# Normalizing half of the Hedgehog features by a ratio of two sums, with other landing margins in the kernel's planner

## The chip, the cores and the metric

The kernel runs on one core of a Trainium2 chip. The metric is the device time of one execution in microseconds (us). Before the change it is 823.11 us, the median of 5 runs that lie between 822.02 and 823.58 us. The profiled execution is one of these runs and took 823.16 us. Its span in the profile, from the first to the last instruction, is 821.4 us, so 1.76 us lie around it.

Names of engines: PE is the matrix engine (PEld its weight loads), ACT the activation engine, DVE the vector engine, POOL the GpSimd engine, SP the engine that issues most transfers.

## The reference: what is computed

One sequence of S = 2048 tokens, width D = 512, H = 32 heads of 16 elements. Two attention branches read the same input `x`, and a gate mixes them: `out = g * a + (1 - g) * b` with `g = sigmoid(sum(x * gate_w))` per token.

- Branch A is ordinary attention: `p = softmax(q k^T / 4)`, `o = p v`, then the output projection. Its 32 x 2048 x 2048 exponentials are most of the work.
- Branch B is linear attention with Hedgehog features. For each head, `pq = q @ w_phi` and `pk = k @ w_phi` have 16 elements. The features are two softmaxes of 16 elements, laid side by side: `phi = [softmax(p), softmax(-p)]`. Then

```python
kv  = einsum("bhsf,bhsd->bhfd", phi_k, v)      # 32 x 16 for each head
z   = phi_k summed over the tokens
num = einsum("bhqf,bhfd->bhqd", phi_q, kv)
den = einsum("bhqf,bhf->bhq", phi_q, z)[..., None] + 1e-6
o   = num / den
```

So each head's feature row has two sums to divide by: s+ of the 16 `exp(p)` and s- of the 16 `exp(-p)`.

## The kernel before, in words

**Branch A, the main chain** (`main_chain`). The work is cut into 32 pieces (a group of four heads and a quarter of the queries), each piece into 16 key tiles of 128 keys, each key tile into four units of 128 keys x 512 queries, one for a head. For two units at a time PE writes scores into two of the four banks of `ps_ring` (line 932), ACT turns them into exponentials in `ET` (line 950, one instruction for 128x1024), and PE multiplies `ET` by the values into `ps_ot` (line 989). The score pair k waits for exponential k-2, because it overwrites its banks. ACT and PE thus run in lockstep with a lead of about one exponential.

**The second way to an exponential** (`dve_pack`). `DVE_COUNT` says for each of the 32 pieces how many of its 16 key tiles don't go to ACT. For such a tile PE writes the scores into a bank of `ps_mp` (line 1039), DVE scales them into a 32-bit integer `EW` (line 1044), POOL or DVE makes the fraction `Ef` of it (line 1073), POOL the exponent part `ED` (line 1077), DVE evaluates a polynomial (lines 1082, 1084, 1086), and an accumulating DMA that POOL issues adds `Ef` to `ED` (line 1089). PE then multiplies `ED` by the values (line 1100). Each such tile takes four units, two exponentials, from ACT.

**Branch B** (`branch_b`, `feature`, `query_b`) runs beside this. For each of 16 token tiles, for keys first and then for queries, `feature` projects (line 773) and ACT writes `exp(p)` and `exp(-p)` into `phi` (line 1241, two instructions). The sums are made by PE: a transposing DMA on SP puts `phi` into `phiT` (line 1260), eight small matmuls with `ind8` give 64 sums for each token (line 1250), DVE takes 64 reciprocals (line 1253) and multiplies all 1024 elements of `phi` (line 1254). For keys, V is projected and copied to `VB` (line 1194) beside a column of ones, eight groups of 65 columns, and PE accumulates `phi^T VB` (line 1204) over four token tiles. For queries `phi` is transposed a second time, PE multiplies it by `kvz` (denominators) and `kvbd` (numerators), and lines 1285, 1288 and 1289 divide. The result is transposed by another DMA into `onT_B` (line 1294).

The three banks of `ps_mp` are shared by all of this: projections, sums, scores for `dve_pack`, and output blocks.

**The order of the work** is not written by hand. When the program is built, a list scheduler (`Sched.run`) plays through all instructions with a table of durations and fixes the order on each engine. Its settings are the lists at the top of the file: due times and leads (`LEAD`, `PACE`, `OFF`, `PRI`, `POLY`), choices for each piece (`PAIR`: scores for `dve_pack` two at a time; `JOINT`: `ET` products of two key tiles together; `SHAPE`, `FILL`, `SHY`, `AFF`, `SLIP`: how the pieces of `dve_pack` are cut and shared between DVE and POOL). PE may take other work ahead of a score pair when `outlook` (line 164) finds that the pair will still be ready in time. For transfers the planner supposes a landing time after the issue; whatever needs the data is placed on PE's queue by it. The actual program waits on semaphores, so a wrong supposition gives no wrong result, but PE takes its queue in order: when a matmul waits for a late transfer, the score pairs behind it wait too. In the planner before, these landing times are

```python
if o.kind == "acc":
    o.end = max([o.start + (5.5 if turns and o.start - turns[-1] < 1.3 else 4.7)] +
                [a.end + 2.65 for a in accs[-1:]])
...
    o.end = o.start + (4.15 if o.kind == "qT" else 3.05 if o.kind == "phi" else 2.43)
```

Here `acc` is the accumulating DMA, `qT` a set of four transfers that place queries (line 808), `phi` and the last one the two transposes of branch B, and `turns` the starts of the transposes. While a product sum in `ps_ot` is open, PE also fills free time with matmuls of zeros (line 1008, `spare_mm`), as long as fewer than `QUOTA` columns were streamed in the last 3.413 us.

Of the kernel before, what the change touches and what calls it, by code (L numbers as in the profile page):

```python
# [8 lines left out]
ALU = mybir.AluOpType  # L9
AX = mybir.AxisListType  # L10

P = 128
D = 512
H = 32
DH = 16
# [16 lines left out]
LEAD = [30.0, 5.0, 15.587634343078882, 18.596008015614277, 21.09664890476773, 40.540151693083416, 4.700229106743385, 13.0]  # L32
PACE = [0.9342151336517385, 0.45790104673263465]
BOUNDS = [3.0710501327799653, 8.000889564597248, 7.98930768224379, 18.02257936663145, 29.86797202712817]
RULES = [0.1498235423970469, 0.5274031413498357, 0.11548542575895482]
# [3 lines left out]
AFF = [4.15497164884861, 0.18343314021531576, 3.4899946808590343, 2.3674940671931393, 0.0, 2.90437474412157, 0.7415344049336196, 3.2417994652524023, 0.0, 0.04936235801504704, 0.5936669881661917, 3.1602669851720693, 0.0, 0.0, 0.44709012098761747, 0.0, 2.1406325166983535, 2.5346731449762023, 0.21204954920410735, 0.0, 3.3400645974699685, 0.22787943080925754, 0.5055877317539534, 0.0, 0.7354200939583246, 2.786126368892715, 1.0743845299433354, 0.7132921107694127, 3.722000841705053, 0.0, 0.0, 0.0, 0.0]  # L39
PAIR = [1, 0, 0, 0, 0, 0, 0, 0, 0, 0, 0, 0, 0, 0, 0, 0, 0, 0, 0, 1, 1, 1, 0, 0, 1, 1, 1, 0, 1, 1, 1, 0, 0]  # L40
JOINT = [0, 0, 1, 1, 0, 1, 0, 1, 1, 0, 1, 0, 1, 0, 0, 1, 1, 0, 1, 0, 0, 0, 0, 1, 0, 0, 1, 0, 0, 0, 1, 0, 0]
SWD = [0.65, 662500, 1.85]
CLEAR = [3.0, 1.2, 0.97]
OFF = [0.0, -0.8897703043510494, 0.5172481291637241, -1.6001482920023302, 2.691800625687394, -4.61876105583856, 9.931835604720934, 3.749480399812751, -2.5354011754586376, 6.457003779301287, 5.486868139035972, -6.13598057955875, 6.241188808437798, -4.516210493380233, -4.720084637924602, 5.808771137792029, -0.362969914738815, 5.451969429638361, -0.20710302246636036, 1.602535412833622, -2.7420692773393607, 6.8960641134545035, -1.5364304379614095, -4.520043988488846, -1.9086060678527623, 4.191789611328016, 0.0, -10.92683283831524, 7.908073056639142, -2.846662271061698, 1.1690496888958446, 2.378092297094616, 0.0]
PRI = [-2.5977761809841518, 12.575398704445774, 3.895376356683779, 11.515588944229506, -9.189983291385724, 11.325175017241945, 6.76640473260813, 12.368950578623885, 19.409552720225648, 1.7122892583984095, -5.057883055897609, 4.784017942556362, 8.536057932420114, 0.1302334100251321, 11.794699785256503, 5.62627294606187, -17.665801839387232, -7.161052481135956, -12.903739516547825, 14.835504297642174, 2.941617488397717, -8.594367097189757, 10.157188453890655, -20.005512559792166, -9.773812266304459, 1.8583573414742158, -5.94449476159381, -2.8717857218875027, -2.836104354426574, -2.8974936905181274, -12.357333215935258, 8.557379841186394, 0.0]
# [4 lines left out]
SHAPE = [0, 2, 0, 2, 2, 1, 0, 0, 2, 2, 1, 0, 0, 0, 0, 0, 0, 0, 0, 1, 0, 1, 2, 0, 0, 0, 2, 1, 1, 1, 1, 1, 1]  # L50
VSL = 17

EC = 0.25 * 1.4426950408889634 * 65536
EM = -68
EU = 0.96498297
E1, E3 = 61.15205816, 9.99312212


DVE_COUNT = (1, 3, 4, 2, 3, 3, 3, 3, 1, 3, 3, 4, 2, 3, 3, 3, 3, 4, 4, 3, 3, 3, 3, 3, 4, 3, 3, 3, 3, 3, 3, 4)


def dve_tiles(n):
    return ((6,), (5, 11), (4, 8, 12), (3, 6, 9, 12), (2, 5, 8, 11, 13))[DVE_COUNT[min(n, NN - 1)] - 1]

# [49 lines left out]
class Sched:  # L124
# [6 lines left out]
    TURN = 0.102  # L131
# [32 lines left out]
    def outlook(self, t, now):  # L164
# [6 lines left out]
        r, back = now, None  # L171
# [1238 lines left out]
```

The softmax here doesn't subtract the row's maximum and nothing guards it: scores larger than these inputs give would overflow.

## Time and profile before

| | |
|---|---|
| median of 5 runs | 823.11 us |
| the profiled execution | 823.16 us |
| its span | 821.4 us |
| granted clock of PE | 1.000 |
| ACT busy | 801.2 us, 98% of the span |
| DVE busy | 775.1 us, 94% |
| PE busy | 770.5 us, 94% (matmuls overlap; fillers included) |
| POOL busy | 412.4 us, 50% |
| `ED<-Ef` issue to landing, median | 4.5 us |
| `phiT<-phi` issue to landing, median | 3.1 us |

A row of a group reads: line, engine, operation, destination and source tile, shape, count, then busy time in us and mean ns of one, then the time for which the engine stood idle just before these instructions and what ended most of it. An instruction's own duration includes its overlap with its neighbours on the engine: an exponential lasts 1157 ns, but they follow each other at 773.9 / 832 = 0.93 us. A row of a timeline gives the start, the length of the merged run, the engine, the line, the count, and in brackets the idle time before it with what ended it. A row of waits gives who waited for what, the total in us, how often, and the longest.

### The profile page before, as it was taken

To read this page: it belongs to the slowest core of one execution; us is meant where nothing else is said; L and a number is where in the kernel's file an instruction comes from. 1 tells how busy PE (TensorE), PEld (TensorE's weight loads), DVE (VectorE), ACT (ScalarE), POOL (GpSimd) and SP (SyncE) were. 2 spreads that over 40 slices of the span, in tenths; PEclk is the share of its full clock that TensorE was granted. 3 is DMA by queue.
4 is the path that set the end of the run, shared out by engine and by line. 5 is a ranking of instruction groups with operands and counts; after the bars stand their busy time and mean duration, and the time that the engine had idled before them with its cause. 6 is when DMAs were issued, how large, how long until landed. Compare 5 with 4: busy or idle time off the path is not lost.

```text
span 821.4 us, 15309 instructions
## 1 busy us (share of the span) xinstructions
PE 770.5 (94%) x6131; PEld 236.2 (29%) x6131; DVE 775.1 (94%) x1093; ACT 801.2 (98%) x904; POOL 412.4 (50%) x493
## 2 busy tenths in 40 slices
PE   8999999999999999988999999999899999899998
PEld 3323333233333232222222222222222222222222
DVE  7999989999999999999999998999999999999994
ACT  6999999999999999999999999999999999999997
POOL 3457446455446544554555454465345456555562
PEclk9999999999999999999999999999999999999999
DMA  6572633445545444455445433455544336534343
GB/s 125 118 123 55 129 61 70 87 90 101 100 107 101 87 93 88 90 107 88 93 101 102 101 74 78 82 92 115 102 91 81 74 73 123 95 75 97 71 97 84
DMA packets 96742, 76.38 MB, mean 93 GB/s; under 512 B 76832, under 2 KB 84384, under 8 KB 96672
## 3 DMA queue, kind: packets, MB, share of 16 engines
q0 software_dynamic: 13824, 50.34, 31.1%
q1 hardware_dynamic: 81504, 24.55, 15.1%
q8 instruction: 48, 0.79, 0.4%
q10 hardware_dynamic: 1344, 0.52, 0.3%
q14 instruction: 22, 0.18, 0.1%
HBM read 3.69 MB, written 2.10 MB: 7 GB/s over the span
## 4 chain that ended last, share of the span: by engine, by line
ACT 70%; PE 11%; DVE 10%; DMA 6%; SPq 1%; issue 1%; POOL 0%; ACTq 0%
ACT ET L950 67%; PE ps_ring L932 4%; DVE EW L1044 3%; DMA ED<-Ef 3%; ACT phi L1241 3%; DMA phiT<-phi 2%; PE ps_ot L989 2%; DVE Ef L1086 1%; DVE Em L1082 1%; DMA qT<-qst 1%; PE ps_mp L773 1%; PE ps_mp L1319 1%; PE ps_mp L1039 1%; SPq L808 1%; DVE phi L1254 1%
## 5 line engine op out<-in xcount | busy, mean ns | idle before, releaser
L950 ACT ACTIVATE ET<-ps_ring 128x1024 bf16<-128x1024 f32 x832 | 773.9, 1157 | 8.6 <-PE ps_ring L932 8.4
L932 PE MATMUL ps_ring<-qT,kT 64*128 64x512 bf16 x1664 | 326.3, 386 | 30.5 <-ACT ET L950 19.7
L1077 POOL TENSOR_SCALAR ED<-EW 128x512 int16<-128x512 int16 (+1 forms) x284 | 232.9, 846 | 172.0 <-DVE Em L1082 62.1
L1044 DVE TENSOR_SCALAR EW<-ps_mp 128x512 int32<-128x512 f32 (+1 forms) x326 | 241.3, 775 | 18.0 <-PE ps_mp L1039 15.2
L932 PEld LDWEIGHTS ps_ring<-qT,kT 64*128 64x128 bf16 x1664 | 80.2, 93 | 296.7 <-ACT ET L950 274.7
L1073 POOL TENSOR_SCALAR Ef<-EW 128x1024 f16<-128x1024 uint16 (+1 forms) x105 | 94.9, 904 | 106.3 <-DVE Ef L1086 36.9
L989 PE MATMUL ps_ot<-ET,Vaug 128*17 128x512 bf16 x1664 | 146.9, 383 | 0.2 <-DVE T L1129 0.2
L1089 POOL DMA_DIRECT2D ED<-Ef x96 | 87.5, 912 | 117.8 <-DVE Ef L1086 65.6
L1082 DVE TENSOR_TENSOR Em<-Ef 128x2048 f16<-128x2048 f16 x96 | 121.5, 1266 | 0.6 <-POOL Ef L1073 0.2
L1008 PE MATMUL ps_ot<-zero,iden 64*128 64x512 bf16 (+2 forms) x570 | 120.7, 377 | 0.0
L1086 DVE TENSOR_TENSOR Ef<-Ef,Em 128x2048 int16<-128x2048 f16 x96 | 120.2, 1252 | 0.3
L1039 PE MATMUL ps_mp<-qT,kT 64*128 64x512 bf16 (+1 forms) x384 | 112.3, 381 | 7.2 <-DMA qT<-qst 2.5
L1073 DVE TENSOR_SCALAR Ef<-EW 128x1024 f16<-128x1024 uint16 (+1 forms) x123 | 75.8, 628 | 0.1
L1084 DVE TENSOR_SCALAR Em<-Em 128x2048 f16<-128x2048 f16 x96 | 71.5, 745 | 0.1
L989 PEld LDWEIGHTS ps_ot<-ET,Vaug 128*17 128x17 bf16 x1664 | 33.4, 87 | 75.9 <-issue 69.7
L1039 PEld LDWEIGHTS ps_mp<-qT,kT 64*128 64x128 bf16 (+1 forms) x384 | 30.0, 94 | 48.0 <-DVE EW L1044 18.6
L773 PE MATMUL ps_mp<-Wp,xT 128*128 128x512 bf16 x128 | 41.2, 384 | 0.1
L1100 PE MATMUL ps_ot<-ED,Vaug 128*17 128x512 bf16 x384 | 37.7, 383 | 3.6 <-DMA ED<-Ef 3.4
L1008 PEld LDWEIGHTS ps_ot<-zero,iden 64*128 64x128 bf16 (+2 forms) x570 | 35.9, 94 | 17.5
L773 PE MATMUL ps_mp<-xT,WA 128*128 128x512 bf16 (+1 forms) x128 | 38.9, 380 | 0.3 <-ACT xT L757 0.3
L1254 DVE TENSOR_TENSOR phi<-phi,ps_mp 128x1024 bf16<-128x1024 bf16 x32 | 38.6, 1208 | 0.4
L1241 ACT ACTIVATE phi<-ps_mp 128x512 bf16<-128x512 f32 x64 | 38.6, 722 | 0.0
(90 smaller groups left out, 401.0 us busy)
## 6 DMA issues: line engine op xcount, KB each, us to landing
ED<-Ef POOLq DMA_DIRECT2D x96, 512.0 KB, 4.5
qT<-qst SPq DMA_DIRECT2D x120, 16.0 KB, 1.8
out_dram<-outt SPq DMA_DIRECT2D x12, 128.0 KB, 1.7
WA<-in_A_wqkv_dram SPq DMA_DIRECT2D x3, 384.0 KB, 4.4
phiT<-phi SPq DMA_TRANSPOSE x48, 3.1
WBV<-in_B_wqkv_dram SPq DMA_DIRECT2D x1, 512.0 KB, 4.3
Wp<-in_A_wo_dram SPq DMA_DIRECT2D x1, 512.0 KB, 3.9
WBV<-in_B_wo_dram SPq DMA_DIRECT2D x1, 512.0 KB, 4.8
```

The costliest lines, as they stand in the source:

```text
L773: m = s.op("pe", self.c_mm(n), lambda e, c=c: e.matmul(self.bk(b)[:, 0:n], lhs(c), rhs(c), start=(c == 0), stop=(c == 3)), deps if c == 0 ...
L932: return lambda e: e.matmul(self.ps_ring[:, x % RING, :], self.kT[r, g // 2, kt * P:(kt + 1) * P], self.qT[r, n % 2, i, :], start=True, st ...
L950: self.o_exp.append(s.op("act", w * 0.434 + 0.039, lambda e, b0=b0, s0=s0, w=w: e.activation(self.ET[:, s0:s0 + w, :], self.ps_ring[:, b0: ...
L989: return lambda e: e.matmul(self.ps_ot[32 * i:32 * i + VSL, :], self.Vaug[:, kt, h, :], self.ET[:, (4 * p + k) % NSLOT, :], start=(kt == 0 ...
L1008: return lambda e: e.matmul(self.ps_ot[c:c + nc, :], self.iden[r:r + nr, 0:nc], self.zero[r:r + nr, :], start=False, stop=False, tile_posi ...
L1039: return lambda e: e.matmul(bank(), self.kT[r, cp, kt * P:(kt + 1) * P], self.qT[r, n % 2, i, :], start=True, stop=True, tile_position=(r. ...
L1044: return s.op("dve", dur, lambda e: e.tensor_scalar(self.EW[:, ew.idx, x * QCH:(x + w) * QCH].rearrange("p (b q) -> p b q", b=w) if w > 1 else
L1073: fs = [s.op("pool", U * 8.26e-4 + 0.28, lambda e, c=c: e.tensor_scalar(self.Ef[:, ef.idx, U * c:U * c + U], half(0, dt.uint16, c, U), flo ...
L1077: hs = [s.op("pool", W * 8.26e-4 + 0.165, lambda e, c=c: e.tensor_scalar(self.ED[:, ed.idx, W * c:W * c + W].bitcast(dt.int16), half(1, dt ...
L1082: u = s.op("dve", 1.13, lambda e: e.tensor_tensor(self.Em[:], Ef(), Ef(), ALU.mult), fs + [self.ed_prev], pr, port=True)
L1086: g_ = s.op("dve", 1.13, lambda e: e.tensor_tensor(Ef().bitcast(dt.int16), Ef(), self.Em[:], ALU.mult), [q], pr, port=True)
L1089: v = s.op("pool", SWD[0], lambda e: e.dma_start(out().bitcast(dt.int16), Ef().bitcast(dt.int16), accum_op=ALU.add), [g_] + hs, pr, frees= ...
```

## The change

In branch B, let s+ and s- be the two sums of a feature row, and r = s- / s+.

- `feature` no longer multiplies all 1024 elements of `phi` by reciprocals. It multiplies only the `exp(p)` half (512 elements) by r, so that both halves lack the same factor 1 / s-. A new small instruction makes r, in free columns of the same bank of `ps_mp`.
- For keys the missing 1 / s- is put on V: the copy to `VB` becomes a multiplication by it, and the column of ones becomes four columns that hold 1 / s- for the four heads of a group (65 columns become 68). So the copy now needs the reciprocals, which stay in a new buffer `rcp` with two slots.
- For queries the factor cancels in num / den, apart from the 1e-6, which is multiplied by s- (new instruction into `sm`) and added together with the gate's factor.
- In the planner the supposed landing times become `CLEAR[3:7]`: 4.85 us for an accumulating DMA, 0.7 us more when a transpose started less than 2.4 us (before: 1.3 us) earlier, 3.26 us for `phi`, 5.2 us for `qT`, 2.6 us for `onT`. `outlook` keeps a further 0.05 us (`CLEAR[7]`) ahead of a score pair, a score pair is costed at 0.2225 instead of 0.2155 us, and `QUOTA` falls from 6000 to 5200 columns.
- `DVE_COUNT` is another list: nine of the 32 pieces change, and the sum goes from 96 to 95 key tiles.
- The settings `AFF`, `PAIR`, `JOINT`, `OFF`, `PRI`, `SHY`, `FILL`, `SLIP`, `POLY` and `SHAPE` get other values for many pieces, and three entries of `LEAD`, `PACE` and `RULES` small changes; these rows are left out below.

```diff
-CLEAR = [3.0, 1.2, 0.97]
+CLEAR = [3.0, 1.2, 0.97, 4.85, 3.2623642462425315, 5.2, 2.6, 0.05]
...
-DVE_COUNT = (1, 3, 4, 2, 3, 3, 3, 3, 1, 3, 3, 4, 2, 3, 3, 3, 3, 4, 4, 3, 3, 3, 3, 3, 4, 3, 3, 3, 3, 3, 3, 4)
+DVE_COUNT = (1, 3, 4, 3, 3, 3, 2, 2, 1, 3, 3, 4, 2, 4, 3, 3, 3, 4, 4, 2, 4, 2, 3, 4, 3, 3, 3, 3, 3, 3, 3, 4)
...
-        return q, r, a - self.TAIL["pe"] - q.dur
+        return q, r, a - self.TAIL["pe"] - q.dur - CLEAR[7]
...
-                    o.end = max([o.start + (5.5 if turns and o.start - turns[-1] < 1.3 else 4.7)] +
+                    o.end = max([o.start + (CLEAR[3] + 0.7 if turns and o.start - turns[-1] < 2.4 else CLEAR[3])] +
                                 [a.end + 2.65 for a in accs[-1:]])
...
-                    o.end = o.start + (4.15 if o.kind == "qT" else 3.05 if o.kind == "phi" else 2.43)
+                    o.end = o.start + CLEAR[{"phi": 4, "qT": 5, "onT": 6}[o.kind]]
...
-    TICK, QUOTA = 3.413, 6000
+    TICK, QUOTA = 3.413, 5200
...
-            o_qk = s.op("pe", 0.2155 if w < 3 else 0.431, [qk(x, w > 1) for x in range(ua, ub + 1)],
+            o_qk = s.op("pe", 0.2225 if w < 3 else 0.431, [qk(x, w > 1) for x in range(ua, ub + 1)],
...
-            o_vb = s.op("dve", self.c_v(512), lambda e, b=b, vb=vb: e.tensor_copy(
-                self.VB[:, vb.idx, :, 0:64], self.bk(b).rearrange("p (g v) -> p g v", v=64)),
-                [m, self.o_vbones], r + 20, frees=[b])
+            low = lambda fs: self.rcp[:, fs.idx].rearrange("p (h s) -> p h s", s=2)[:, :, 1]
+            o_vz = s.op("dve", 0.1, lambda e, vb=vb, fs=fs, low=low: e.tensor_copy(
+                self.VB[:, vb.idx, :, 64:68], low(fs).rearrange("p (g a) -> p g a", a=4)),
+                [rc], r + 20, alloc=[vb], frees=[fs], port=True)
+            o_vb = s.op("dve", 0.605, lambda e, b=b, vb=vb, fs=fs, low=low: e.tensor_tensor(
+                self.VB[:, vb.idx, :, 0:64].rearrange("p g (a d) -> p g a d", d=DH),
+                self.bk(b).rearrange("p (g a d) -> p g a d", a=4, d=DH),
+                low(fs).rearrange("p (g a) -> p g a", a=4)[:, :, :, None].to_broadcast([P, 8, 4, DH]), ALU.mult),
+                [m, rc, o_vz], r + 20, frees=[b, fs])
...
-        rc = s.op("dve", 0.475, lambda e: e.reciprocal(self.bk(b2)[:, 0:64], self.bk(b2)[:, 0:64]), [m], r + 10)
-        sc = s.op("dve", 1.13, lambda e: e.tensor_tensor(
-            flat(), flat(), self.bk(b2)[:, 0:64, None].to_broadcast([P, 64, DH]), ALU.mult), [rc], r + 10,
-            frees=[b2])
-        return ph, sc
+        sums = lambda k: self.bk(b2)[:, 0:64].rearrange("p (h s) -> p h s", s=2)[:, :, k]
+        if qk:
+            fs = Buf(self.fs_p, 3)
+            rc = s.op("dve", 0.475, lambda e: e.reciprocal(self.rcp[:, fs.idx, :], self.bk(b2)[:, 0:64]), [m], r + 10,
+                      alloc=[fs])
+            inv = lambda: self.rcp[:, fs.idx].rearrange("p (h s) -> p h s", s=2)[:, :, 0]
+            more, fr = (fs, rc), [fs]
+        else:
+            fs = Buf(self.fs_p, 1)
+            rc = s.op("dve", 0.27, lambda e: e.reciprocal(self.rcp[:, fs.idx, 0:32], sums(0)), [m], r + 10, alloc=[fs])
+            inv = lambda: self.rcp[:, fs.idx, 0:32]
+            sm = s.op("dve", 0.12, lambda e: e.tensor_scalar(
+                self.sm[:, t % 2, :], sums(1), 1e-6, self.gpos[:, t:t + 1], op0=ALU.mult, op1=ALU.mult),
+                [m, self.o_gpos, self.sm_last.get(t - 2)], r + 10, frees=[b2])
+            more, fr = (sm,), [fs]
+        ro = s.op("dve", 0.12, lambda e: e.tensor_tensor(
+            self.bk(b2)[:, 96:128], inv(), sums(1), ALU.mult), [rc], r + 10, frees=fr)
+        sc = s.op("dve", 0.605, lambda e: e.tensor_tensor(
+            self.phi[:, ph.idx, :, 0, :], self.phi[:, ph.idx, :, 0, :],
+            self.bk(b2)[:, 96:128, None].to_broadcast([P, H, DH]), ALU.mult), [ro], r + 10, frees=[b2])
+        return (ph, sc, *more)
...
-        z1 = s.op("dve", 0.16, lambda e: e.tensor_scalar(
-            rz(), self.bk(bs[0])[:, 0:32], 1e-6, self.gpos[:, t:t + 1], op0=ALU.add, op1=ALU.mult),
-            [mm[0], self.o_gpos], r + 22, frees=[bs[0]])
+        z1 = s.op("dve", 0.16, lambda e: e.scalar_tensor_tensor(
+            rz(), self.bk(bs[0])[:, 0:32], self.gpos[:, t:t + 1], self.sm[:, t % 2, :], op0=ALU.mult, op1=ALU.add),
+            [mm[0], self.o_gpos, o_sm], r + 22, frees=[bs[0]])
```

Where the order of the whole program is built for both kernels, the instruction counts change as follows: exponentials on ACT (line 950 before) 832 to 834; accumulating DMAs 96 to 95; line 1044 with 1024 elements 58 to 74 and with 512 elements 268 to 232; line 1073 on DVE with 1024 elements 91 to 105 and with 512 elements 32 to 24; line 1073 on POOL 65 to 63 and 40 to 20; line 1077 on POOL with 1024 elements 100 to 114 and with 512 elements 184 to 152; fillers of line 1008 from 570 to 502 matmuls (310 to 278 of the wide forms, 260 to 224 of the narrow one). The orders of the two kernels are the same for the first 145 matmuls and differ from there to the end.

## The prediction

> **What bounds the kernel.** I read the page's busy shares, then ACT's waits, then the timeline of ACT, then PE's timeline ahead of each gap that ACT shows.
>
> ```profile
> ACT ET L950 <- PE ps_ring L932: 8.4, 16, 1.9
> ```
>
> ```profile
> L950 ACT ACTIVATE ET<-ps_ring 128x1024 bf16<-128x1024 f32 x832 | 773.9, 1157 | 8.6 <-PE ps_ring L932 8.4
> L932 PE MATMUL ps_ring<-qT,kT 64*128 64x512 bf16 x1664 | 326.3, 386 | 30.5 <-ACT ET L950 19.7
> ```
>
> ```profile
> 10.01 56.02 ACT L950 ACTIVATE ET<-ps_ring 128x1024 bf16<-128x1024 f32 x61 [1.87 <-PE ps_ring L932]
> ...
> 317.41 12.94 ACT L950 ACTIVATE ET<-ps_ring 128x1024 bf16<-128x1024 f32 x14 [0.68 <-PE ps_ring L932]
> 331.01 1.02 ACT L950 ACTIVATE ET<-ps_ring 128x1024 bf16<-128x1024 f32 x1 [0.66 <-PE ps_ring L932]
> ...
> 703.58 110.38 ACT L950 ACTIVATE ET<-ps_ring 128x1024 bf16<-128x1024 f32 x120 [0.72 <-PE ps_ring L932]
> 816.99 1.26 ACT L1360 ACTIVATE outz<-ps_mp,gcol 128x512 bf16<-128x512 f32 x2 [3.02 <-PE ps_mp L1319]
> ```
>
> ACT is the bound: from its first exponential at 10.01 us to the end of the last at 703.58 + 110.38 = 813.96 us it is almost never idle. At their tightest the exponentials follow each other every 0.917 us: 120 of them in 110.38 us, the last one 1.157 us long, give (110.38 - 1.16) / 119 = 0.918, other undisturbed runs of the timeline 0.915 to 0.918. A pair of feature exponentials takes 0.98 us in the chain. Undisturbed, the stretch would be 832 x 0.917 + 32 x 0.98 + 0.13 (the two gate exponentials) = 794.4 us. It is 803.95. So 9.5 us are lost in it: 6.5 us in 15 waits for scores (8.4 less the first 1.87 us), and 3.0 us in gaps too short to be listed. Head (10.0 us) and tail (7.4 us) hold no instruction that the change edits.
>
> Why the scores were late stands on PE's queue, ahead of the score pair that ended ACT's wait:
>
> ```profile
> 316.65 0.39 PE L1100 MATMUL ps_ot<-ED,Vaug 128*17 128x512 bf16 x4 [1.10 <-DMA ED<-Ef]
> 316.98 0.39 PE L932 MATMUL ps_ring<-qT,kT 64*128 64x512 bf16 x2
> ```
>
> ```profile
> 383.85 0.60 PE L1039 MATMUL ps_mp<-qT,kT 64*128 64x512 bf16 x3 [1.09 <-DMA qT<-qst]
> 384.08 0.58 PE L932 MATMUL ps_ring<-qT,kT 64*128 64x512 bf16 x2
> ```
>
> Eight of the 15 waits are of this sort: a matmul ahead of the scores waits for a transfer. ACT loses 0.45 + 0.68 + 0.49 us behind ED (at 265, 317 and 353 us), 0.66 + 0.56 + 0.18 behind qT (331, 385, 435), 0.18 + 0.63 behind phiT (562, 582): 3.8 us. The other seven, 2.65 us, are matmuls that wait for DVE or POOL (0.28 at 76, 0.50 at 284, 0.15 at 488, 0.72 at 704: 1.65) or simply too many matmuls between two score pairs (0.44, 0.17, 0.39: 1.0).
>
> **Part 1, one key tile goes back to ACT.** The 32 counts sum to 95 instead of 96, so ACT gets two more exponentials, on the path: 2 x 0.917 = +1.83 us. This is certain.
>
> **Part 2, landing times.** I compare how late PE's matmul was with what the planner's supposition is raised by. A consumer placed later by the margin waits that much less.
> - qT, raised by 1.05 us. PE waited 0.78, 1.09 and 0.63 us; after it 0, 0.04 and 0. Gain 0.66 + 0.56 + 0.18 = 1.40.
> - ED, raised by 0.15, and by 0.85 (4.7 to 5.55) where a transpose started 1.3 to 2.4 us earlier. At 265 us it did (transpose at 257.71, DMA at 259.31): the wait of 0.61 goes, gain 0.45. At 317 us (DMA at 310.61, the transpose before it at 306.20) and 353 us only 0.15 each is gained: 0.30. There landing took 6.0 and 5.9 us, still beyond 4.85.
> - phiT, raised by 0.21: PE's 0.54 and 0.94 us become 0.33 and 0.73, ACT gains 0.18 + 0.21 = 0.39.
> Sum: -2.5 us. It holds if the new order has no more such collisions than the old; bounds are a gain of 3.8 (all eight gone) and a loss of as much (as many more).
>
> **Part 3, work on DVE and POOL.** Neither is the bound, but a late DVE is behind four of the waits.
> Removed in branch B: 32 multiplications of 1024 elements (38.6 us), 32 reciprocals of 64 (17.6), 16 copies to VB (11.0): 67.2 us. Added: 32 multiplications of 512 elements, between half of the 1024 (0.60 us) and the nearest row, 128x512 from a PSUM bank with a broadcast factor in line 1289 (10.8 / 16 = 0.675), 19.3 to 21.6; 32 ratios of 32 elements at 0.23 (line 1285) 7.4; 16 sm, the same, 3.7; reciprocals 16 x 0.55 + 16 x 0.335 (line 1288) = 14.2; 16 scaled copies at 0.675, 10.8; 16 copies of 32 elements at 0.16 (line 730) 2.5. Sum 57.9 to 60.2, so DVE saves 7 to 9 us there.
>
> ```profile
> L1254 DVE TENSOR_TENSOR phi<-phi,ps_mp 128x1024 bf16<-128x1024 bf16 x32 | 38.6, 1208 | 0.4
> ...
> L1289 DVE TENSOR_TENSOR ob<-ps_mp,rz 128x512 bf16<-128x512 f32 x16 | 10.8, 678 | 0.1
> ```
>
> The new shares of the second way's work come out even: one polynomial less, (121.5 + 71.5 + 120.2) / 96 = -3.3; EW 16 x 1.217 - 36 x 0.637 = -3.4; Ef 14 x 0.694 - 8 x 0.394 = +6.6. DVE falls from 775 to about 767 us, 1%. POOL loses 22 us: 14 x 1.10 - 32 x 0.67 - 2 x 1.08 - 20 x 0.615 - 0.9 - 0.6. I take half of the 1.65 us of waits for DVE and POOL as gone, -0.8; bounds -1.65 and, since all orders are new, +1.65.
>
> **Part 4, the 0.05 us ahead of a score pair, and fewer fillers.** 0.05 us each time PE has other work to place bears on the 3.0 us of short gaps and on the three waits of 1.0 us. No row prices it; all gone is -4.0, none is 0, and a tighter packing elsewhere could cost as much as it gains. I take -1.0, nearer to none, since PE has the same work to place between the score pairs: by the counts of both orders 5563 matmuls without fillers before and after. The 68 fillers fewer, 32 x 0.307 + 36 x 0.095 = 13 us of PE's busy time, stand only in PE's free time, so 0. That holds while the clock does: every stretch of 50 us shows it granted at 1.00, with PE busy 45.1 us or more.
> [...] Without any of its 120.7 us of fillers PE would still be busy (770.5 - 120.7) / 821.4 = 79%, which I don't call idle. [...]
>
> **Part 5, the new waits.** The copy to VB waits for the reciprocals, holding one of the three banks of ps_mp meanwhile; behind it on DVE stand EW conversions, and for the bank the scores of line 1039. In the new program's order the V projection stands behind the sums of its token tile in 15 of 16 cases, so the reciprocals are done first: 0, the cover being PE's order. z1 waits for sm, which was issued a whole transpose (3.1 us) earlier: 0. The kv products go from 65 to 68 columns: 128 x 3 columns at 512 per 0.217 us (line 1319 in the tail: four of them in 1.04 us, the last 0.385 long) is 0.2 us of PE, in its free time. The tail has one matmul set of ED (0.2 us) earlier: -0.2 at most, taken as 0.
>
> **Sum:** 823.16 + 1.83 - 2.5 - 0.8 - 1.0 = 820.7 us against the profiled execution, which is 0.05 above the median. Limits of the likeliest case: 822.5 (part 2 alone) and 818.
>
> **Rivals.**
> - No change: the margins work as costed, the rest of the new order brings nothing. 823.16 + 1.83 - 2.5 = 822.5, and to 824.5 when half of part 2 is lost to new collisions. For it: ED's two longest landings stay outside the margin, and DVE stays at 93% of the span.
> - Large gain: nearly all of the 9.5 us go. 823.16 + 1.83 - 9.5 = 815.5 is the floor; with a third left, 818.5 down to 816. For it: each wait's cause is one that a truer planner avoids. Against: 2.65 us of waits and 3.0 us of short gaps have causes that no landing time touches.
> - Slower: the bank that V holds. If the reciprocals come late, a tile of dve_pack gets its bank late, its ED lands late, and PE waits ahead of a score pair. At the mean of the eight transfer waits, 3.8 / 8 = 0.48 us, for each of 16 key tiles it is +7.7 us: 823.16 + 1.83 - 2.5 + 7.7 = 830. At 0.15 us for each key tile the forecast's gain is gone; from 0.26 us it is slower by over 0.2%. Against it: the order above, and 0.8 us in all that VB's copy waited before. At half the price it ends near 826.5.
> - The change doesn't do what it says: if the half multiplication costs as much as the whole one (1.2 us), DVE gains nothing, and 32 x 0.6 = 19 us more stand on DVE. It still has over 30 us idle, so I put this within the slower case.
>
> **Chances.** A measurement of this kernel tells about 0.2%, 1.65 us, from no change. Forecast (818 to 821.5) 0.42, large gain 0.16, no change 0.17, slower 0.25 (of which a good half below 827). Faster 0.58, same 0.17, slower 0.25. The range leaves out the last part of the slow case and the floor: 816.2 to 826.8.
>
> **What would show it.** ACT's waits for scores: 834 exponentials, waits from 8.4 to about 4.5 us, none behind qT, one or two behind ED and phiT. Half multiplications of 0.60 to 0.68 us, DVE busy 767, POOL 390, PE 757, clock 1.00. Wrong: waits of line 1039 for DVE's VB between 85 and 235 us, ED still landing 5.5 us or more with PE waiting, a clock below 1.00, or short gaps above 3 us.

## The result, and the profile after

The changed kernel takes 821.1 us, the median of 36 runs (819.92 to 824.08); the kernel before, run beside it, 823.85 us (62 runs, 820.64 to 828.77). The ratio is 0.9965, 95% interval 0.9957 to 0.9974: 0.26 to 0.43% faster. The forecast of 820.7 us and the range of 816.2 to 826.8 held. Of its terms, though, the two exponentials and the margins for qT and phiT did what was said of them, as far as that can be told, the margin for ED did not, the lighter DVE can't be had as a term of its own, and the fillers, which were set to zero, turned out to be large.

Single runs of one kernel differ by some us. That goes with PE's granted clock, whose mean over a run of these two kernels was between 0.991 and 1.000: in the changed kernel the 13 runs at 1.000 have a median of 820.58 us, the 24 below it one of 821.63 us. So medians are compared, and in each experiment the ratio is to the kernel before as run in the same group on the same chip.

The profiled execution took 821.29 us, its span is 819.4 us, the clock 0.998.

| | before | after |
|---|---|---|
| exponentials of the chain | 832 | 834 |
| first starts, last ends | 10.01, 813.96 us | 9.34, 812.27 us |
| the stretch between | 803.95 us | 802.93 us |
| the same, undisturbed (as in the prediction) | 794.4 us | 796.2 us |
| lost in listed waits | 6.5 us | 5.2 us |
| lost in gaps too short to be listed | 3.0 us | 1.5 us |
| DVE, POOL, PE busy | 775.1, 412.4, 770.5 us | 765.3, 396.7, 766.7 us |
| fillers (matmuls) | 570 | 502 |

The 2.0 us between the two spans are 1.0 us of the stretch, 0.3 us of the tail (7.44 to 7.13 us) and 0.7 us of the head. The head's work is the same, and its length varies: in the profiles of the experiments below the first exponential starts between 9.33 and 10.40 us.

ACT's waits for scores:

```profile
ACT ET L952 <- PE ps_ring L934: 5.1, 8, 1.9
```

They fell from 16 to 8. Where they stand is in ACT's timeline:

```profile
9.34 56.02 ACT L952 ACTIVATE ET<-ps_ring 128x1024 bf16<-128x1024 f32 x61 [1.86 <-PE ps_ring L934]
...
68.84 2.85 ACT L952 ACTIVATE ET<-ps_ring 128x1024 bf16<-128x1024 f32 x3 [0.58 <-PE ps_ring L934]
72.36 13.04 ACT L952 ACTIVATE ET<-ps_ring 128x1024 bf16<-128x1024 f32 x14 [0.66 <-PE ps_ring L934]
...
147.24 1.08 ACT L1250 ACTIVATE phi<-ps_mp 128x512 bf16<-128x512 f32 x2 [1.94 <-PE ps_mp L775]
...
549.52 1.02 ACT L952 ACTIVATE ET<-ps_ring 128x1024 bf16<-128x1024 f32 x1 [1.23 <-PE ps_ring L934]
550.72 9.44 ACT L952 ACTIVATE ET<-ps_ring 128x1024 bf16<-128x1024 f32 x10 [0.17 <-PE ps_ring L934]
...
702.16 110.11 ACT L952 ACTIVATE ET<-ps_ring 128x1024 bf16<-128x1024 f32 x120 [0.21 <-PE ps_ring L934]
```

The pitch of the undisturbed chain is the old one (120 exponentials in 110.11 us). What is left: two waits behind late ED (68 and 72 us, 1.24 us), one in front of a pair of feature exponentials that stands too early in ACT's order (147 us, 1.94 us), and 1.40 us at 549 us. PE's waits for transfers, before and then after:

```profile
PE ps_ot L1100 <- DMA ED<-Ef: 3.4, 5, 1.1
PE ps_mp L1039 <- DMA qT<-qst: 2.5, 3, 1.1
PE ps_mp L1250 <- DMA phiT<-phi: 2.4, 4, 0.9
```

```profile
PE ps_ot L1102 <- DMA ED<-Ef: 3.1, 6, 1.0
...
PE ps_mp L1259 <- DMA phiT<-phi: 0.2, 1, 0.2
```

The row for qT is gone, phiT nearly so, ED is as it was. The wait at 549 us is of another kind. These rows of the window view give start and end of a stretch, its length, then busy time (and instruction count) of PE, PEld, DVE, ACT and POOL, then PE's granted clock, the DMA share and GB/s:

```profile
544.29:547.70 3.41, 2.33 (x29) 1.08 (x26) 3.41 (x5) 3.41 (x5) 1.51 (x2) 1.00 0.85 169
547.70:551.11 3.41, 3.20 (x32) 1.01 (x32) 2.67 (x8) 2.01 (x3) 2.99 (x3) 0.50 0.55 109
```

PE has little to do for some 3 us (small products of 4 and 64 columns, and waits of 0.27, 0.50 and 0.53 us for ACT, DVE and ED). Then it runs at half clock for 3.41 us: the score matmuls of line 934 take 603 to 606 ns each there, 386 to 387 ns in the 7 us before. So the scores are not late only because ED was late: in the profile of a_q6000 below, the same matmuls with the same waits (0.27, 0.51 and 0.56 us) ran at a clock of 1.00 throughout, and there ACT waited 0.64 us instead of 1.40.

### The profile page after: what moved, and what is told of

Same layout as the page of the kernel before. It is cut to its first block, busy times and chain, and to the rows that moved or that the text cites. A ratio compares the mean times of both kernels' runs of the same rounds, so it can differ in the third digit from the quotient of the medians.

```text
span 819.4 us, 15193 instructions
## 1 busy us (share of the span) xinstructions
PE 766.7 (94%) x6063; PEld 231.5 (28%) x6063; DVE 765.3 (93%) x1140; ACT 801.5 (98%) x906; POOL 396.7 (48%) x451
## 4 chain that ended last, share of the span: by engine, by line
ACT 73%; DVE 13%; PE 9%; DMA 3%; issue 1%; POOL 1%; ACTq 0%; SPq 0%; POOLq 0%
ACT ET L952 70%; DVE EW L1046 4%; ACT phi L1250 3%; DMA ED<-Ef 3%; PE ps_ring L934 3%; DVE Em L1084 2%; DVE Ef L1088 2%; PE ps_mp L775 2%; DVE Ef L1075 1%; PE ps_ot L991 1%; DVE Em L1086 1%; PE ps_mp L1041 1%; PE ps_mp L856 1%; POOL ED L1079 0%; PE ps_ot L1102 0%
## 5 line engine op out<-in xcount | busy, mean ns | idle before, releaser
L1046 DVE TENSOR_SCALAR EW<-ps_mp 128x512 int32<-128x512 f32 (+1 forms) x306 | 238.0, 809 | 16.4 <-PE ps_mp L1041 14.9
L991 PE MATMUL ps_ot<-ET,Vaug 128*17 128x512 bf16 x1668 | 149.0, 384 | 0.9 <-DVE T L1131 0.8
L1075 POOL TENSOR_SCALAR Ef<-EW 128x1024 f16<-128x1024 uint16 (+1 forms) x83 | 79.3, 955 | 86.6 <-DVE EW L1046 19.8
L1041 PE MATMUL ps_mp<-qT,kT 64*128 64x512 bf16 (+1 forms) x380 | 108.4, 380 | 2.9 <-DVE EW L1046 1.2
L1010 PE MATMUL ps_ot<-zero,iden 64*128 64x512 bf16 (+2 forms) x502 | 107.9, 377 | 0.0
L1075 DVE TENSOR_SCALAR Ef<-EW 128x1024 f16<-128x1024 uint16 (+1 forms) x129 | 83.1, 654 | 0.2
L1250 ACT ACTIVATE phi<-ps_mp 128x512 bf16<-128x512 f32 x64 | 40.3, 776 | 1.9 <-PE ps_mp L775 1.9
L1010 PEld LDWEIGHTS ps_ot<-zero,iden 64*128 64x128 bf16 (+2 forms) x502 | 32.0, 94 | 15.6
L1131 DVE STREAM_TRANSPOSE T<-ps_ot 128x512 f32<-128x512 f32 x31 | 21.9, 708 | 4.3 <-PE ps_ot L991 4.0
```

Source lines behind the costliest of these rows:

```text
L991: return lambda e: e.matmul(self.ps_ot[32 * i:32 * i + VSL, :], self.Vaug[:, kt, h, :], self.ET[:, (4 * p + k) % NSLOT, :], start=(kt == 0 ...
L1010: return lambda e: e.matmul(self.ps_ot[c:c + nc, :], self.iden[r:r + nr, 0:nc], self.zero[r:r + nr, :], start=False, stop=False, tile_posi ...
L1041: return lambda e: e.matmul(bank(), self.kT[r, cp, kt * P:(kt + 1) * P], self.qT[r, n % 2, i, :], start=True, stop=True, tile_position=(r. ...
L1046: return s.op("dve", dur, lambda e: e.tensor_scalar(self.EW[:, ew.idx, x * QCH:(x + w) * QCH].rearrange("p (b q) -> p b q", b=w) if w > 1 else
L1075: fs = [s.op("pool", U * 8.26e-4 + 0.28, lambda e, c=c: e.tensor_scalar(self.Ef[:, ef.idx, U * c:U * c + U], half(0, dt.uint16, c, U), flo ...
```

## The experiments

### Fixed orders: what a single cause is worth

In the first group the planner's order is kept and a single thing in it is changed.

**b_swap.** The order before, with eight score pairs put ahead of the matmul that waits for a transfer.

```diff
                 self.s.run()
+                for k, j in ((255, -1), (309, -1), (323, -1), (344, 0), (377, 0), (429, 0), (564, -8), (583, -8)):
+                    ahead(self.s.out, self.s.chain[k], slot(self.s, k)[j])
```

(`slot` lists PE's other work ahead of score pair k, `ahead` moves the pair in front of one of it.)

> The kernel before, with the same order but for eight places: there the score pair is put ahead of the matmul that waits for a transfer (ED at 265, 317, 353 us, qT at 331, 385, 435, phiT at 562, 582). Theory (ACT is the bound, and PE's queue stands before late transfers): ACT's eight waits, 3.8 us in all, go; 3 to 3.8 us faster, waits for scores from 8.4 to about 4.6 us. Rival (DVE sets the end, ACT's waits are made good later): within 0.5 us of before, with other waits in place of these.

Measured: 822.24 us, ratio 0.9981 (0.9963 to 0.9998). ACT's timeline no longer shows the waits at 265, 317, 331, 353 and 562 us, 2.46 us in all, and the one at 582 us fell from 0.63 to 0.23 us. The one at 385 us stayed (0.80 us, before 0.56), and the one at 435 us (0.18 us before) grew to several:

```profile
384.90 32.19 ACT L975 ACTIVATE ET<-ps_ring 128x1024 bf16<-128x1024 f32 x35 [0.80 <-PE ps_ring L957]
...
435.92 1.02 ACT L975 ACTIVATE ET<-ps_ring 128x1024 bf16<-128x1024 f32 x1 [1.28 <-PE ps_ring L957]
437.20 1.02 ACT L975 ACTIVATE ET<-ps_ring 128x1024 bf16<-128x1024 f32 x1 [0.26 <-PE ps_ring L957]
```

At 434 to 437 us the clock was 0.55. So a late transfer ahead of a score pair does cost ACT time, as the prediction read it, but the kernel won 1.1 us by medians (0.2 to 3.0 by the interval), about a third of the 3.8 us that the eight waits add up to and under half of the five that went.

**b_two.** The order before, with two exponentials done twice, to measure what a key tile on ACT costs.

```diff
+                for j, (k, ua) in enumerate(((630, 1260), (770, 1540))):
+                    o = self.o_exp[k]
+                    o.fns = [lambda e, j=j, b0=ua % RING: e.activation(
+                        self.twice[:, 2 * j:2 * j + 2, :], self.ps_ring[:, b0:b0 + 2, :], ACT.Exp,
+                        scale=float(DH) ** -0.5)] + o.fns
```

> The kernel before in its own order, with two of its exponentials of 128x1024 done twice (the first time into a spare tile), at about 620 and 755 us. Theory: two exponentials more cost 2 x 0.917 = 1.8 us, as part 1 of the prediction has it. Rival: ACT has slack that takes them, under 0.5 us.

Measured: 825.5 us, ratio 1.0011 (0.9990 to 1.0032); 2.15 us above the kernel before by medians. The +1.83 us of part 1 lies inside the interval, and so does the rival's 0 to 0.5 us; these runs can't tell the two apart.

**b_half.** The order before, with the multiplication of `feature` on 512 elements instead of 1024: 17 us less on DVE.

```diff
-            flat(), flat(), self.bk(b2)[:, 0:64, None].to_broadcast([P, 64, DH]), ALU.mult), [rc], r + 10,
+            self.phi[:, ph.idx, :, 0, :], self.phi[:, ph.idx, :, 0, :],
+            self.bk(b2)[:, 0:32, None].to_broadcast([P, H, DH]), ALU.mult), [rc], r + 10,
```

> The kernel before in its own order, but the multiplication of phi covers the first 512 of 1024 elements. Left out: the normalization of the exp(-p) half, and the factors of the other half are not the right ones. DVE gets 32 x 0.53 = 17 us less work, twice what the change takes from it. Theory: DVE is not the bound; at most 1 us faster. Rival (the lighter DVE is where the change's gain comes from): 3 us faster or more.

Measured: 825.63 us, ratio 1.0021 (0.9998 to 1.0044). No gain at all. Where the clock stayed at 1.000 the medians are 823.27 and 823.22 us.

**a_full.** The reverse in the new order: all 1024 elements again, 17 us more on DVE.

```diff
-            self.phi[:, ph.idx, :, 0, :], self.phi[:, ph.idx, :, 0, :],
-            self.bk(b2)[:, 96:128, None].to_broadcast([P, H, DH]), ALU.mult), [ro], r + 10, frees=[b2])
+            flat(), flat(), self.bk(b2)[:, 0:64, None].to_broadcast([P, 64, DH]), ALU.mult), [ro], r + 10,
+            frees=[b2])
```

> The order of the changed kernel, but the multiplication in feature takes all 1024 elements again (by the plain sums, so the normalization is left out); 32 x (1.21 - 0.67) = 17 us more on DVE, ratios and sums still made. If a lighter DVE is worth something in this order (part 3 of the prediction took 0.8 us for it), the kernel loses 0.8 to 3 us against the changed one (ratio 0.9975 to 1.000). Rival: DVE's waits hide it, as in the old order, where 17 us less brought nothing: within 0.5 us of the changed kernel (ratio 0.996 to 0.997). Second rival: each late multiplication delays a bank and a product behind it, +5 us or more (ratio over 1.002).

Measured: 831.1 us, ratio 1.0096 (1.0078 to 1.0114), 10 us above the changed kernel. The second rival was right. ACT's waits for scores:

```profile
ACT ET L952 <- PE ps_ring L934: 10.4, 19, 1.9
```

They doubled against the changed kernel (5.1 us, 8 times). PE's timeline shows a piece of it, a product of branch B that waits for DVE ahead of a score pair:

```profile
553.88 0.60 PE L1303 MATMUL ps_mp<-kvbd,phiT 128*128 128x64 bf16 x8 [1.09 <-DVE EW L1046]
```

From 553.9 to 560.8 us the clock was 0.50, and the score pairs that start at 554.41, 556.48 and 557.67 us took 0.61 us, the one at 552.40 us 0.39. So a part of the 10 us may come by way of the clock; these runs don't separate it. Together with b_half: in these two fixed orders, time taken off DVE was worth nothing, and time put on it cost more than half of itself. That an order is cut for the durations it was planned with would explain both.

**a_early.** The order of the changed kernel; in eight places the first matmul that needs a new qT stands two score pairs earlier, 1.2 to 1.4 us, which takes the margin back.

```diff
                 self.s.run()
+                out, chain = self.s.out, self.s.chain
+                for k in (35, 253, 276, 429, 582, 685, 737, 789):
+                    i = out.index(chain[k])
+                    x = next(o for o in out[i + 1:] if o.eng == "pe" and o not in chain and any(
+                        d.kind == "qT" for d in o.deps))
+                    ahead(out, x, chain[k - 1])
```

> The order of the changed kernel, with the first matmul that needs a new qT put two score pairs earlier in eight places (some 1.2 to 1.4 us earlier, which takes back the 1.05 us of margin and a little more). If the margin for qT is what ended ACT's waits behind qT (part 2 of the prediction, 1.40 us), three or four of the eight places wait again, 0.4 to 0.7 us of ACT each: 1.2 to 2.5 us slower than the changed kernel (ratio 0.998 to 0.9995), and PE's waits for qT of 2 us or more stand in the profile. Rival: the data lands earlier in this order anyway and the margin has no part in the gain: within 0.4 us of the changed kernel.

Measured: 823.61 us, ratio 1.0011 (0.9994 to 1.0027); 2.5 us above the changed kernel by medians, at the upper end of what was expected. PE waited for qT at 428 us (0.50), at 725 us (1.63) and once ahead of a score pair (0.6). The one at 725 us, on PE, then on ACT:

```profile
725.23 0.39 PE L1070 MATMUL ps_mp<-qT,kT 64*128 64x512 bf16 x2 [1.63 <-DMA qT<-qst]
```

```profile
725.90 1.02 ACT L981 ACTIVATE ET<-ps_ring 128x1024 bf16<-128x1024 f32 x1 [1.45 <-PE ps_ring L963]
727.18 2.10 ACT L981 ACTIVATE ET<-ps_ring 128x1024 bf16<-128x1024 f32 x2 [0.26 <-PE ps_ring L963]
729.54 1.02 ACT L981 ACTIVATE ET<-ps_ring 128x1024 bf16<-128x1024 f32 x1 [0.26 <-PE ps_ring L963]
731.46 86.28 ACT L981 ACTIVATE ET<-ps_ring 128x1024 bf16<-128x1024 f32 x94 [0.90 <-PE ps_ring L963]
```

```profile
722.00:725.40 3.40, 1.25 (x14) 0.32 (x14) 3.40 (x7) 2.46 (x3) 0.20 (x1) 1.00 0.83 161
725.40:728.80 3.40, 3.40 (x17) 1.00 (x14) 2.62 (x3) 2.59 (x3) 1.53 (x2) 0.54 0.00 0
728.80:732.20 3.40, 3.40 (x18) 0.56 (x16) 1.16 (x1) 2.24 (x3) 1.23 (x2) 0.50 0.49 98
```

PE waits 1.63 us; ACT loses 1.45 us at once and 0.26 + 0.26 + 0.90 = 1.42 us more in the 6.8 us at half clock that follow. The profiled run is the slowest of the 12 (826.73 us), so this is the dear case. In the four runs with a clock of 1.000 the median is 822.39 us, still 1.8 us above the changed kernel's 820.58 in its runs with that clock. So the margin for qT does what the prediction said (the move is somewhat larger than the margin), and here a wait of 1.63 us on PE, with 6.8 us at half clock behind it, cost ACT 1.45 + 1.42 = 2.87 us.

### Fillers and the clock

**a_fill.** The order of the changed kernel with five fillers more, at 545 to 548 us, where PE had little to do ahead of the wait at 549 us.

```diff
                 self.s.run()
+                out = self.s.out
+                for k, n in ((551, 1), (552, 2), (553, 2)):
+                    i = out.index(self.s.chain[k]) + 1
+                    for _ in range(n):
+                        z = self.s.spare("H")
+                        z.start = z.end = z.ready = out[i - 1].start
+                        out.insert(i, z)
```

> The changed kernel in its own order, with five filler matmuls more between 545 and 548 us, where its profile shows PE with small matmuls and waits, and after it a stretch of 3.4 us at half the clock and 1.4 us of waits of ACT. Theory (too little matmul work there lets the clock fall): clock 1.000, the wait at 549 us at most 0.4 us, and about 0.7 us faster than the changed kernel, ratio to before near 0.9955. Rival (the late ED transfer and DVE make that wait): the wait stays above 1 us and the ratio at 0.9965, whatever the clock.

Measured: 820.83 us, ratio 0.9960 (0.9941 to 0.9979), 0.3 us below the changed kernel, which can't be told from nothing. The wait at 549 us fell from 1.40 to 0.43 us. In this profile the half clock came later instead:

```profile
573.00:576.00 3.00, 1.87 (x14) 0.50 (x18) 3.00 (x5) 3.00 (x5) 0.79 (x1) 0.90 0.67 137
576.00:579.00 3.00, 3.00 (x20) 0.62 (x12) 2.75 (x6) 2.29 (x3) 1.50 (x3) 0.53 0.39 76
```

So the fillers took most of the wait at 549 us away, but only a part of that is theirs for certain: in a_q6000, without these five fillers, the wait was 0.64 us in a run whose clock stayed up. That its removal is worth anything isn't shown.

**a_nofill.** The order of the changed kernel without any filler.

```diff
                 self.s.run()
+                self.s.out[:] = [o for o in self.s.out if o not in spares]
```

(`spares` collects what `spare_mm` made.)

> The order of the changed kernel with all its fillers left out (107.9 us of PE's busy time), nothing else moved. The prediction's part 4 holds fillers for free time: PE is then still busy (766.7 - 107.9) / 819.4 = 80% of the span, the clock stays at 1.00 and the time within 1 us of the changed kernel's (ratio 0.995 to 0.998). Rival, from the half-clock stretch seen at 548 us after some 3 us with PE 50 to 60% busy: without fillers such stretches come all over the program; mean clock below 0.98, ten or more waits of the score pairs beside them, and at 1.5 us each or more a time of 835 us or above (ratio over 1.013).

Measured: 834.89 us, ratio 1.0154 (1.0122 to 1.0187), 13.8 us above the changed kernel; the clock is 0.957 in the profile and 0.94 to 0.97 in the others. Stretches of 40 us late in the program:

```profile
650.00:690.00 40.00, 30.73 (x247) 8.64 (x249) 38.35 (x56) 39.63 (x46) 20.38 (x26) 0.96 0.47 92
690.00:730.00 40.00, 32.06 (x242) 8.48 (x239) 36.37 (x48) 39.15 (x43) 25.50 (x31) 0.86 0.45 89
730.00:770.00 40.00, 30.85 (x210) 7.01 (x212) 34.71 (x40) 38.32 (x42) 17.30 (x25) 0.80 0.35 69
```

The rival was right: PE is still busy three quarters of the time, and its clock falls. Read in steps of 1.70 us from 10 to 807 us, it is below 1.00 in 13 places, by the rows 3.4, 6.8 or 13.6 us at 0.50 each, 71.6 us in all, which is 21 times 3.41 us. One such 3.41 us takes 1.7 / 40 = 0.0425 off the mean of a row above, so these rows hold about one, three and five of them; over the whole program the missing clock, 0.043 x 833 = 36 us, is 21 times 1.7. 13.8 us divided by 21 are 0.65 us for each, an estimate that puts all of the loss down to them: by it, most of the 1.7 us of each is hidden behind ACT.

**a_q6000.** The changed kernel with the old quota: the order of all other work is identical, 49 fillers more.

```diff
-    TICK, QUOTA = 3.413, 5200
+    TICK, QUOTA = 3.413, 6000
```

> The changed kernel with the old QUOTA of 6000 columns: the order of all other work is identical, 49 more fillers. If the smaller quota costs nothing (the prediction's part 4), the ratio is that of the changed kernel, 0.9965, within 0.001. If more fillers keep the clock up, the granted clock is 1.000 in more than half of its runs and the time 0.3 to 1 us lower (ratio 0.9955 or less). If fillers stand in the way of score pairs, it is 0.5 us or more slower (ratio 0.997 or above).

Measured: 823.43 us, ratio 1.0007 (0.9994 to 1.0021). That is 2.3 us above the changed kernel by medians and 0.42% by ratios, 0.26 to 0.58% with the uncertainty of both: the third of the three expectations. With the old quota the changed kernel would be no faster than the kernel before. The changed kernel was not run beside it, and the kernel before was quicker in this group (822.51 us) than in the others (823.35 and 823.99 us), so of the two figures I trust the smaller one more. What the fillers cost can't be read from the profile: the profiled run is one of the quickest (821.87 us, clock 1.000), and its stretch is 803.34 us, 0.4 us above the changed kernel's. PE's waits for transfers, though, are 5.8 us in it, where the changed kernel has 3.3, and the row for qT is back:

```profile
PE ps_ot L1102 <- DMA ED<-Ef: 4.5, 8, 1.2
...
PE ps_mp L1041 <- DMA qT<-qst: 1.1, 2, 0.6
```

More fillers didn't hold the clock up: its mean over the runs is 0.9975, in the changed kernel 0.9985. Nor does the clock seem to be the main way by which they cost: in the three runs at 1.000 the median is 822.23 us, 1.65 us above the 820.58 us of the changed kernel's 13 such runs. By which way 49 fillers cost 2 us stays open.

### New plans: one setting put back

In these three a single part of the change is undone, and the planner makes a new order with all other settings of the changed kernel.

**a_oldland.** The old landing times.

```diff
-CLEAR = [3.0, 1.2, 0.97, 4.85, 3.2623642462425315, 5.2, 2.6, 0.05]
+CLEAR = [3.0, 1.2, 0.97, 4.7, 3.05, 4.15, 2.43, 0.05]
...
-                    o.end = max([o.start + (CLEAR[3] + 0.7 if turns and o.start - turns[-1] < 2.4 else CLEAR[3])] +
+                    o.end = max([o.start + (CLEAR[3] + 0.8 if turns and o.start - turns[-1] < 1.3 else CLEAR[3])] +
```

> The changed kernel, all its settings kept, planned with the landing times of before (4.7 and 5.5 within 1.3, 3.05, 4.15 and 2.43 us); the 0.05 us ahead of a score pair stay. The planner orders everything anew after the start. Theory (the margins carry the gain): PE waits for transfers as in the kernel before, ACT's listed waits rise by 2 us or more, ratio to before 0.999 to 1.002. Rival (the margins are not what carries it): within 1 us of the changed kernel, 0.9955 to 0.9975.

Measured: 839.54 us, ratio 1.0180 (1.0149 to 1.0211).

**a_nolead.** Without the 0.05 us, and score pairs costed at 0.2155 us.

```diff
-CLEAR = [3.0, 1.2, 0.97, 4.85, 3.2623642462425315, 5.2, 2.6, 0.05]
+CLEAR = [3.0, 1.2, 0.97, 4.85, 3.2623642462425315, 5.2, 2.6, 0.0]
...
-            o_qk = s.op("pe", 0.2225 if w < 3 else 0.431, [qk(x, w > 1) for x in range(ua, ub + 1)],
+            o_qk = s.op("pe", 0.2155 if w < 3 else 0.431, [qk(x, w > 1) for x in range(ua, ub + 1)],
```

> The changed kernel, all its settings kept, planned without the 0.05 us ahead of a score pair and with 0.2155 us for one, as before; the landing times stay new. Theory (part 4: they shorten ACT's gaps that are too short to be listed): these gaps go from 1.5 back to about 3 us, 1 to 1.5 us slower than the changed kernel, ratio to before 0.9975 to 0.9985. Rival: the short gaps stay at 1.5 us.

Measured: 838.93 us, ratio 1.0182 (1.0152 to 1.0212).

**a_oldfeat.** Branch B's arithmetic as before (the last three hunks of the diff undone, with their buffers), planner and settings as after.

> The changed kernel's planner and settings with branch B's arithmetic of before (whole multiplication of phi, a copy to VB, a column of ones). DVE gets 7 to 9 us more work. Theory (DVE is not the bound): within 1 us of the changed kernel, ratio to before 0.996 to 0.9985. Rival (the lighter DVE is what lets the planner avoid waits): 3 us slower than the changed kernel or more, above 1.000.

Measured: 844.7 us, ratio 1.0242 (1.0214 to 1.0269). The largest of its waits on ACT:

```profile
ACT ET L950 <- PE ps_ot L989: 15.6, 6, 6.8
```

This is a kind of wait that neither kernel has: an exponential waits for a slot of `ET` because PE's products are far behind, up to 6.8 us at a time. It stands in a_oldland too (7.2 us in 4) and in a_nolead (6.9 us in 5). The theories missed the time in all three by 13 us or more. Of the rivals only that of a_oldfeat holds by its number (above 1.000), but runs that leave DVE's work as it is came out nearly as slow, so it isn't thereby shown. The likeliest reason for all three is that the settings of the 32 pieces are fitted to one exact table of durations and landing times, and that any part put back alone gives an order that nobody fitted, here 18 to 24 us above the changed kernel; no run tests this reason. So these runs don't say what the part itself is worth, and only the fixed orders above do.

### A version meant to be better

**a_best.** The order of the changed kernel with three fillers ahead of 549 us, five score pairs ahead of products of ED that came late, and one exponential ahead of the feature exponentials at 147 us.

```diff
                 self.s.run()
+                out = self.s.out
+                for k, n in ((551, 1), (552, 2)):
...
+                for k in (64, 67, 554, 584, 714):
+                    x = next(o for o in slot(self.s, k) if o.kind is None and o.cfg == "C" and any(d.kind == "acc" for d in o.deps))
+                    ahead(out, self.s.chain[k], x)
+                ahead(out, self.o_exp[141], out[out.index(self.o_exp[140]) + 1:][next(
+                    i for i, o in enumerate(out[out.index(self.o_exp[140]) + 1:]) if o.eng == "act")])
```

> The changed kernel in its own order, with three fillers at 545 to 547 us, five score pairs put ahead of the ED matmul that waits in its profile (68, 72, 549, 580, 702 us), and one exponential put ahead of the feature exponentials that waited 1.94 us at 147 us. Theory (ACT's bound is lost only to these waits): 0.58 + 0.66 + 0.9 + up to 1.4 + 0.4 us less; since moving scores in the kernel before gave a third to a half of the sum of its waits, 1.5 to 2.5 us faster than the changed kernel, ratio to before 0.9935 to 0.995. Rival (waits only move): 0.996 to 0.9975.

Measured: 821.68 us, ratio 0.9960 (0.9942 to 0.9978): as the changed kernel. The waits at 549, 580 and 702 us are gone, the two for ED are about as long, and the exponential that was moved waits itself:

```profile
148.63 1.02 ACT L987 ACTIVATE ET<-ps_ring 128x1024 bf16<-128x1024 f32 x1 [2.27 <-PE ps_ot L1026]
...
152.42 1.02 ACT L987 ACTIVATE ET<-ps_ring 128x1024 bf16<-128x1024 f32 x1 [0.87 <-PE ps_ring L969]
153.93 8.47 ACT L987 ACTIVATE ET<-ps_ring 128x1024 bf16<-128x1024 f32 x9 [0.48 <-PE ps_ring L969]
```

Its slot in `ET` comes free behind a product that PE does later, so 1.94 us of waiting became 2.27 + 0.87 + 0.48 = 3.62 us, the last two of them at half clock (0.50 from 150.7 to 154.1 us; the mean from 110 to 160 us is 0.97). No version here beats the changed kernel by more than the noise.

## Why the prediction was right, and where it was not

**Part 1**, +1.83 us for two exponentials: right as far as it can be told (b_two: +2.15 by medians, with 0 inside its interval; the pitch of the chain is unchanged).

**Part 2**, -2.5 us. qT, -1.40: right. PE's waits for qT are gone, and a_early, which moves their consumers 1.2 to 1.4 us earlier, brings them back with 2.5 us. phiT, -0.39: right, 0.2 us of waits are left of 2.4 and ACT loses nothing there. ED, -0.75: wrong. The three places that were read are gone with their order, but the new order has ED late in others; PE waits 3.1 us in 6 where it waited 3.4 in 5, and landings take up to 6.8 us, beyond a margin of 4.85 or 5.55. This is the case that part 2 named as its condition, new collisions for old ones. b_swap shows besides that a wait's length is not its price: five waits of 2.46 us went, others grew, and 1.1 us was won.

**Part 3.** The durations were right or a little high: half multiplication 0.673 us (forecast 0.60 to 0.68), ratio 0.188 (0.23), reciprocals 0.547 and 0.333 (0.55, 0.335), scaled copy 0.679 (0.675). DVE is busy 765 us (767), POOL 397 (390).

```profile
L1279 DVE TENSOR_TENSOR phi<-phi,ps_mp 128x512 bf16<-128x512 bf16 x32 | 21.5, 673 | 0.2
...
L1201 DVE TENSOR_TENSOR VB<-ps_mp,rcp 128x512 bf16<-128x512 f32 x16 | 10.9, 679 | 2.3 <-PE ps_mp L775 2.3
...
L1277 DVE TENSOR_TENSOR ps_mp<-rcp,ps_mp 128x32 f32<-128x32 f32 x32 | 6.0, 188 | 0.5
```

The price of it, -0.8, is not a term that can be added: b_half gives 0 for twice the saving in an order planned for the slow form, a_full +10 in an order planned for the fast one. The rival that the half multiplication might cost as much as the whole, which was put at no more than the slower case because DVE has over 30 us idle, would have been 831 us: that is a_full.

**Part 4.** The short gaps fell from 3.0 to 1.5 us, near the -1.0 that was taken; that the 0.05 us did it is not shown, since a_nolead made a new plan. The step that failed is that the fillers "stand only in PE's free time, so 0. That holds while the clock does". It was argued from stretches of 50 us, all with a clock of 1.00 in that one profile. But in other runs the clock of the kernel before is below 1.000 too (in 25 of 35 runs, down to 0.991), and fillers were not free in either direction: of the 68 fewer 49 came with the quota; these 49 put back cost 2.3 us, as far as groups run on different chips can be compared, and all 502 taken out cost 13.8 us. With the old quota the whole change came to about nothing against the kernel before on the same chip (ratio 1.0007, 0.9994 to 1.0021), where the prediction had -2.5 us without it. Such prices don't add up: a_early loses the whole gain too, by the margin for qT alone. A stretch of 3.41 us at half clock cost 0.65 us on average in a_nofill, by the estimate there, and the 6.8 us behind the wait in a_early 1.42 us. The gain itself is mostly not one of the clock: in runs at 1.000 the median of the kernel before is 822.12, 822.42 and 823.22 us in the three groups of the experiments (9, 6 and 10 runs), 1.5 to 2.6 us above the changed kernel's 820.58.

**Part 5**, new waits at 0: right. The copy to VB waited 2.3 us in all, for its own projection (row L1201 above), not for the reciprocals; `sm` held up nobody. The rival of the slower side, V holding its bank, did not come.

**Not foreseen:** 1.94 us at 147 us, where ACT's order has the feature exponentials ahead of their projection. So the balance of the profiled run is 1.83 - 1.3 (listed waits) - 1.5 (short gaps) = -1.0 us in the stretch, against -2.5; the medians differ by 2.7. Two of the signs of being wrong that the prediction named did appear: ED landed after up to 6.8 us with PE waiting, and the clock was below 1.00 (0.998 in the profile, below 1.000 in 24 of 37 runs). PE was busy 767 us instead of 757, although the fillers' own time fell as counted, from 120.7 to 107.9 us; where the other 9 us come from stays open. So the total was right partly by luck, by a composition that was another one: too much from ED and DVE, nothing from the quota.

## What to carry to other kernels

A wait in a profile is a place, not a price: of eight that were moved out of the way five went, one grew where the clock was 0.55, and a third of their length was won; and one long wait, in the slowest run of its kernel, cost nearly twice its length (1.63 us on PE, 2.87 us on ACT). Where an order is planned from a table of durations, test a part of a change at a fixed order; putting one entry of the table back measures a new plan. And of filler work there was too little here with none (13.8 us lost) and, as far as one pair of quotas shows, too much with 49 matmuls more (2.3 us lost): ask of it in both directions, and look at the clock in steps of a few us and over several runs, since the 3.41 us at 0.50 in the changed kernel leave the mean from 510 to 560 us at 0.97.

## What the runs showed of the hardware

- **PE's clock fell to 0.50 behind stretches in which PE had work.** In the changed kernel PE was busy 2.33 of the 3.41 us ahead of the half clock (the row of 544.29 us above), in a_early 1.25 of the 3.40 us from 722.00 us (the clock is 0.54 and 0.50 in the two rows behind it), in a_nofill 3.22 of the 5.10 us from 747.80 us (the clock is 0.50 from 752.90 us). In a_nolead it was busy all the time, with 75 matmuls:

```profile
58.82:62.23 3.41, 3.41 (x75) 2.09 (x74) 2.00 (x3) 3.41 (x5) 1.28 (x3) 1.00 0.02 5
62.23:65.64 3.41, 2.99 (x16) 0.68 (x17) 1.65 (x3) 2.73 (x3) 3.13 (x5) 0.50 0.55 112
```

- **The same program ran with half clock and without it.** The changed kernel's mean clock was 1.000 in 13 of its 37 runs, 0.995 to 0.999 in the other 24. In a_q6000, with the same order of all other work and 49 fillers more, the matmuls that ran at half clock in the changed kernel from 547.70 us ran at 1.00:

```profile
543.58:546.99 3.41, 2.64 (x29) 0.89 (x27) 3.41 (x5) 3.41 (x5) 2.67 (x3) 1.00 0.73 143
546.99:550.41 3.42, 2.85 (x46) 1.31 (x46) 3.13 (x7) 2.78 (x4) 1.93 (x2) 1.00 0.34 69
```

  PE's busy time alone does not tell when the clock falls: around the wait for qT at 383 us in the kernel before, PE was busy 2.21 of the 3.42 us from 382.35 us, a little less than the 2.33 of 3.41 us named above, and the clock is 1.00 there and in the 3.41 us behind. What else decides it is not shown.
- **Half clock cost less than it took from PE** where ACT is the bound: 3.41 us at 0.50 are 1.7 us of full clock, and 21 such stretches in a_nofill cost 13.8 us, 0.65 us each by the estimate there. In a_early, where PE was already late by a wait of 1.63 us, ACT lost 1.42 us in the 6.8 us at half clock.
